# Linear attention and a gated feed-forward layer on one core: weight sums, two loads and the order of block 1 moved to other places

## The chip, the cores and the metric

The kernel runs on one core of a Trainium2 chip. The metric is the device time of one execution in microseconds (us), lower is better. The engines named here are PE (TensorE: matmuls and transposes through the array), DVE (VectorE), ACT (ScalarE), POOL (GpSimd, which also issues DMAs on a queue of its own, q0 in the profile) and SP (SyncE, which only issues DMAs, on queue q1).

## The reference

```
attention, batch 8, heads 8, sequence 576, head size 64:
  phi(x) = [relu(x) * cos(w_pos), relu(x) * sin(w_pos)]      (128 features)
  kv = sum over s of phi(k)_s v_s^T ;  z = sum over s of phi(k)_s
  x  = (phi(q) kv) / (phi(q) z + 1e-6)
feed-forward on the 8 * 576 = 4608 rows of x:
  h = x @ w_in            (512 -> 2048)
  y = (h * sigmoid(1.702 h)) @ w_out      (2048 -> 512)
```

Inputs and output are float32; the kernel multiplies in bfloat16.

## The kernel before

**Blocks.** Each batch b is one block. Its first 512 positions go through the feed-forward layer in the block itself; the last 64 positions of every batch are kept in `xt` and `gt` and done together behind the last block. The instructions of each engine are written out by hand in the order in which they run, so whatever stands ahead on an engine's list and waits holds back all that follows on that engine.

**What one block does.** `load_q`, `load_kv` bring q, k and v of a batch into the single buffers `qf`, `kf`, `vf` (about 1.2 MB each). DVE makes phi(q) into `qn` (`trig_q`, L185, ten instructions) and SP turns it into `qT` by five transposing DMAs (`qturn_dma`, L219). DVE makes phi(k) into `kr` (`trig`, L169, eighteen instructions) and copies v into `vt` (`vcopy`, L193). `kv_next` multiplies `kr` and `vt` on PE (L237, 72 small matmuls) and DVE takes the result out into `kvs` (L245). `x_next(b, c)` makes the attention output of one chunk c of the positions: `num_mm` on PE (L310, needs `kvs` and `qT`), `num_div` on DVE (L321, L323, L325), and a transposing DMA into `xT`. `mm1(b, fc)` is the first matmul of the layer (L365, four matmuls of 512 columns, sixteen fc to a block), followed by the activation on ACT (L371).

**The second matmul of the layer.** Block 0 uses plain matmuls (`mm2`, L419). From block 1 on it is done by seven products in place of eight (`wino_mm`, L502). Those need four sums of quarters of w_out, kept in `wsum` (`w_sums`, L440 to L443: t1, t2, t3, nt4), and sums of quarters of the activations (`g_sums`, L465 to L471). t1 reads the first half of w_out alone, the other three read the second half too.

**Order around the change.** In block 0, POOL issues the loads q of batch 1, the third quarter of w_out, v of batch 1 and the last quarter of w_out. DVE makes phi(k) and phi(q) of batch 1 and half of `vcopy`; ACT does the rest of both. SP issues the five transposes of `qT`, then q, k and v of batch 2, in that order on one queue. PE runs `mm2(0, ...)`, and from the middle of its last quarter on `kv_next`, `num_mm(0)` to `num_mm(4)` of batch 1. Then DVE makes the four weight sums in one go, ahead of all its work for batch 2.

In block 1 the first five `mm1` are done in `start_block`, so the loop starts at fc 5. Blocks 2 to 6 place `kv_next` for the next batch in front of `mm1(b, 14)` and `x_next(b + 1, 0)` in front of the products. Block 1 alone places `vcopy` behind the second step of the products, `kv_next` behind step 3, and the five `x_next` behind steps 4, 5, 6, 8 and 10.

Of the kernel before, what the change touches and what calls it, by code (L numbers as in the profile page):

```python
# [15 lines left out]
SUB = mybir.AluOpType.subtract  # L16
# [4 lines left out]
def kernel(  # L21
# [9 lines left out]
    nc = tc.nc  # L31
# [25 lines left out]
    def src_of(src, b, i0=0, i1=NI):  # L57
        return src[b, 2 * i0:2 * i1].rearrange("(i hh) (p j) d -> (hh p) i (j d)", hh=2, j=NS)

    qf = one.tile([128, 2560], F32, name="qf")  # L60
    kf, vf = [one.tile([128, NI, S], F32, name=n) for n in ("kf", "vf")]
# [62 lines left out]
    def load(t, src, b, eng=nc.gpsimd):  # L124
        eng.dma_start(out=t, in_=src_of(src, b))

    def load_chunks(t, src, b, eng):
        eng.dma_start(out=t[:, 0:2048].rearrange("p (h e) -> p h e", h=H),
                      in_=src[b, :, 0:512, :].rearrange("h (p c) d -> p h (c d)", c=4))
        eng.dma_start(out=t[0:64, 2048:2560].rearrange("p (h e) -> p h e", h=H),  # L130
                      in_=src[b, :, 512:S, :].rearrange("h p d -> p h d"))

    def load_q(b, eng=nc.gpsimd):
        load_chunks(qf, q, b, eng)
# [11 lines left out]
    def load_kv(b):  # L146
        load(kf, k, b, nc.sync)
        load(vf, v, b, nc.sync)
# [12 lines left out]
    def trig(dst, src, j, act=False, eng=nc.vector):  # L161

        i = src[:, :, ts(j, 64)]
        for cs, w in enumerate((cosw, sinw)):
            o = dst[:, j, :, ts(cs, 64)]
            if act is True or (act == "sin" and cs == 1):
                nc.scalar.activation(o, i, AF.Relu, scale=w[:, j:j + 1])
            else:
                eng.tensor_scalar(o, i, 0.0, w[:, j:j + 1], op0=MAX, op1=MUL)  # L169
# [6 lines left out]
    def trig_q(c, act=False):  # L176
        n = 128 if c < 4 else 64
        i = chunk(qf, c)
        for cs, w in enumerate((cosw, sinw)):
            o = qn[0:n, c, :, ts(cs, 64)]  # L180
            sc = w[0:n, NS + c:NS + c + 1]
            if act:
                nc.scalar.activation(o, i, AF.Relu, scale=sc)
            else:
                nc.vector.tensor_scalar(o, i, 0.0, sc, op0=MAX, op1=MUL)  # L185

    def vcopy(i0=0, i1=NI, act=False):
        o = vt[:, :, i0:i1, 0:64].rearrange("p j i e -> p i j e")
        i = vf[:, i0:i1].rearrange("p i (j e) -> p i j e", e=64)
        if act:  # L190
            nc.scalar.activation(o, i, AF.Copy)
        else:
            nc.vector.tensor_copy(o, i)  # L193
# [23 lines left out]
    def qturn_dma(c):  # L217
        n = 128 if c < 4 else 64
        nc.sync.dma_start_transpose(out=qT[:, :, c * 128:c * 128 + n],  # L219
                                    in_=qn[0:n, c].rearrange("p h f -> p (h f)"))  # L220
# [3 lines left out]
    def kv_open(i0=0, i1=NI, n=65):  # L224
        t = pat.tile([128, 2, 512], F32, name="at")
        for i in range(i0, i1):
            st["kv", i] = t[:, :, ds((i - i0) * n, n)]
        st["ps", i0] = t[:, :, 0:(i1 - i0) * n]
        if i0 == 0:
            st["kvs"] = small.tile([128, 2, NI, VW], BF16, name="kvs", bufs=2)  # L230

    def kv_mm(i0, i1, rhs, col, n):
        for i in range(i0, i1):
            for j in range(NS):
                for hh in range(2):
                    r = slice(hh * 64, hh * 64 + 64)
                    nc.tensor.matmul(st["kv", i][:, hh, ds(col, n)], kr[r, j, i, :], rhs(r, i, j),  # L237
                                     start=(j == 0), stop=(j == NS - 1))
# [4 lines left out]
    def kv_evac(i0, i1, n=65):  # L243
        o = st["kvs"][:, :, i0:i1, 0:n]
        nc.vector.tensor_copy(o, st["ps", i0].rearrange("p hh (i e) -> p hh i e", e=n))  # L245
# [85 lines left out]
    def x_open(b):  # L331
        x[b] = xpool.tile([128, KC, MT], BF16, name="xT")
# [40 lines left out]
    def mm1(b, fc):  # L373
        mm1_part(b, fc, 0, MT)
        gelu(fc)
# [38 lines left out]
    def mm2(b, t, lo, hi, c0=0, c1=d_model, end=False):  # L414
# [6 lines left out]
        if hi == FC:  # L421
# [10 lines left out]
    wt = {n: wsum[:, i].rearrange("p (f d) -> p f d", f=HF)  # L432
          for i, n in enumerate(("t1", "t2", "t3", "nt4"))}
    wq = {(k, n): w_out_sb[:, ts(k, HF), ts(n, HD)] for k in range(2) for n in range(2)}
    sg = {n: sums[:, i].rearrange("p (f t) -> p f t", f=HF)
          for i, n in enumerate(("s1", "s2", "s3", "s4"))}

    def w_sums():
        tt = nc.vector.tensor_tensor
        tt(wt["t1"], wq[0, 1], wq[0, 0], op=SUB)  # L440
        tt(wt["t2"], wq[1, 1], wt["t1"], op=SUB)
        tt(wt["t3"], wq[1, 1], wq[0, 1], op=SUB)
        tt(wt["nt4"], wq[1, 0], wt["t2"], op=SUB)  # L443

    def main_blk(i, qd):

# [11 lines left out]
    def g_sums(names, h, of=MAIN):  # L458

        tt = nc.vector.tensor_tensor  # L460
        a_blk, to = of
        o = {n: to[n][:, ts(h, 4)] for n in to}
        for n in names:
            if n == "s1":
                tt(o[n], a_blk(1, h), a_blk(1, h + 2), op=ADD)  # L465
            elif n == "s2":
                tt(o[n], o["s1"], a_blk(0, h), op=SUB)  # L467
            elif n == "s3":
                tt(o[n], a_blk(0, h), a_blk(1, h), op=SUB)  # L469
            else:  # L470
                tt(o[n], a_blk(0, h + 2), o["s2"], op=SUB)  # L471
# [117 lines left out]
    def kv_next():  # L589
        kv_open()  # L590
        kv_mm(0, 4, vt_rhs, 0, 65)
        kv_evac(0, 4)
# [122 lines left out]
    load_wout(3)  # L715
    for j in range(NS):
        trig(kr, kf, j)
    for fc in range(8, FC):
        mm1(0, fc)
    mm1_tail_first(0)  # L720
    mm1_tail_first(1)
    for c in range(5):
        trig_q(c, act=(c > 2))
        qturn_dma(c)
    vcopy(0, 2)
    vcopy(2, 4, act=True)
    load_q(2, nc.sync)
    load_kv(2)
    for g in range(2):
        for t in range(4):  # L730
            mm2(0, t, 4 * g, 4 * g + 4)
# [21 lines left out]
    def kv_operands(b):  # L753
        for j in range(NS):
            trig(kr, kf, j)
        if b > 2:
            vcopy()

    def x_next(b, c):
        num_mm(c)  # L760
        num_div(c)
        xturn_dma(b, c)


    w_sums()

    for b in range(1, B):
        nb = b + 1 if b + 1 < B else None
        f0 = 5 if b == 1 else 0
        for fc in range(f0, FC):  # L770
            if nb is not None and fc == f0:
                for c in range(5):
                    trig_q(c)
                    qturn_dma(c)
            if nb is not None and fc == f0 + 1:
                kv_operands(nb)

                if nb + 1 < B:
                    load_q(nb + 1, nc.sync)
            if fc == 12:  # L780
                g_sums(("s3",), 0)
                g_sums(("s3",), 1)
                g_sums(("s1", "s2", "s4"), 0)
            if fc == 14 and nb is not None and b > 1:
                kv_next()
            mm1(b, fc)
        if nb is not None:
            x_open(nb)
            if b > 1:
                x_next(nb, 0)  # L790
            g_sums(("s1", "s2"), 1)
            at = {2 * p + 1: [p + 1] for p in range(4)} if b > 1 else {4: [0], 5: [1], 6: [2], 8: [3], 10: [4]}
            wino_open()
            for p in range(7):
                for c in range(2):
                    wino_mm(p, c)
                    s = 2 * p + c
                    if c == 1:
                        wino_after(b, p)
                    if s == 3 and b == 1:  # L800
                        kv_next()
                    for c2 in at.get(s, ()):
                        x_next(nb, c2)
                        if c2 == 3 and nb + 1 < B:
                            load_kv(nb + 1)
                    if s == 1:
                        g_sums(("s4",), 1)
                        if b == 1:
                            vcopy()
            continue  # L810
        for fc in range(FC):
            mm1_tails(fc)
            if fc == 0:
                g_sums(("s1", "s2", "s4"), 1)
        for h in range(2):
            g_sums(("s1", "s2"), h, TAIL)
        g_sums(("s3",), 0, TAIL)
        g_sums(("s3",), 1, TAIL)
        wino_open()
        for p in range(7):  # L820
            for c in range(2):
                wino_mm(p, c, TAIL)
            wino_after(None, p, end=True)
            if p == 1:
                g_sums(("s4",), 0, TAIL)
                g_sums(("s4",), 1, TAIL)
        wino_open(last=True)
        for p in range(7):
            for c in range(2):
                wino_mm(p, c)  # L830
                if p == 6:
                    wino_last(b, c)
            wino_after(b, p, end=True)
# [30 lines left out]
```

## Time and profile before

| what | value |
|---|---|
| time, median of 3 runs (lowest, highest) | 286.5 us (285.62, 286.88) |
| the profiled execution: its own time, its span | 288.89 us, 287.2 us |
| PE busy, share of the span | 273.7 us, 95% |
| DVE, ACT, POOL busy | 185.7, 128.3, 41.4 us |
| mean granted clock of PE | 0.987 |
| DMA packets on q1 (SP), q0 (POOL), share of 16 engines | 56.8%, 20.2% |

Busy times are sums over an engine's instructions. The span runs from the first to the last instruction; the execution's own time has what lies around it as well. "Idle before" is time in which an engine had nothing to run ahead of a group, and the name behind the arrow ended that wait. A DMA's time to landing runs from its issue until its data is there.

### The profile page before, as it was taken

The numbers are of one execution on the slowest core, as the hardware profiler recorded it, in microseconds if no ns is written. First come the engines' busy times: TensorE is split into PE (matmuls) and PEld (weight loads), VectorE is DVE, ScalarE is ACT, GpSimd is POOL, SyncE is SP. The second block draws the span as 40 slices with busy tenths as digits, with TensorE's granted clock in tenths as the row PEclk, the third lists the DMA queues.
The fourth block names the chain that finished last, engine by engine and source line by source line (L and its number), as shares of the span: only waits on it lengthen the run. The fifth ranks groups of instructions, "written<-read, shape, count | busy, mean of one in ns | idle before, by whom it ended". The sixth has DMA issues, their size and how long they took to land.

```text
span 287.2 us, 6573 instructions
## 1 busy us (share of the span) xinstructions
PE 273.7 (95%) x2700; PEld 191.5 (67%) x2700; DVE 185.7 (65%) x451; ACT 128.3 (45%) x225; POOL 41.4 (14%) x70
## 2 busy tenths in 40 slices
PE   8999999996698989999999999999999999999995
PEld 2675645854594559757975797579757975568884
DVE  4835434799585798796779678967897711516111
ACT  6967543672014722364236413641374137773221
POOL 5680003200112001300130013001300130000320
PEclk9999999999599999999999999999999999999999
DMA  7999999999349999999699979987994430000143
GB/s 238 245 212 295 270 257 204 350 296 202 103 64 251 290 183 168 292 264 236 112 305 221 217 148 314 256 212 107 290 279 54 109 119 2 0 0 2 47 138 110
DMA packets 73661, 53.57 MB, mean 187 GB/s; under 512 B 52736, under 2 KB 63488, under 8 KB 73632
## 3 DMA queue, kind: packets, MB, share of 16 engines
q1 hardware_dynamic: 67504, 36.97, 56.8%
q0 software_dynamic: 6128, 16.19, 20.2%
q8 instruction: 21, 0.34, 0.5%
q14 instruction: 8, 0.07, 0.1%
HBM read 36.70 MB, written 9.44 MB: 161 GB/s over the span
## 4 chain that ended last, share of the span: by engine, by line
PE 77%; DVE 10%; DMA 9%; issue 1%; ACT 1%; POOL 0%; DVEq 0%; SPq 0%
PE mm L502 32%; PE mm L365 29%; DMA kf<-in_k_dram 5%; PE mm L396 4%; PE mm L419 4%; PE at L237 3%; DVE kr L169 3%; PE at L310 3%; DMA sums<-in_v_dram 2%; DMA out_dram<-ysb 2%; DVE qn L185 1%; DVE vt L193 1%; DVE sums L469 1%; PE mm L388 1%; DVE sums L467 1%
## 5 line engine op out<-in xcount | busy, mean ns | idle before, releaser
L365 PE MATMUL mm<-xT,w_in 128*128 128x512 bf16 (+1 forms) x592 | 113.7, 349 | 1.5 <-DMA xT<-xn 1.4
L371 ACT ACTIVATE g<-mm 128x512 bf16<-128x512 f32 x128 | 75.6, 598 | 41.2 <-PE mm L365 41.2
L365 PEld LDWEIGHTS <-w_in 128*128 128x128 bf16 x592 | 60.1, 113 | 48.3 <-issue 1.7
L502 PEld LDWEIGHTS <-sums 128*128 128x128 bf16 x448 | 42.6, 98 | 5.0
L508 POOL DMA_DIRECT2D out_dram<-ysb x24 | 17.5, 729 | 165.2 <-DVE inv L323 96.8
L502 PE MATMUL mm<-wsum,sums 128*128 128x256 bf16 x336 | 40.9, 276 | 0.0
L502 PEld LDWEIGHTS <-g 128*128 128x128 bf16 x336 | 32.2, 98 | 3.8
L169 DVE TENSOR_SCALAR kr<-kf,cosw 128x256 bf16<-128x256 f32 x69 | 24.2, 350 | 10.0 <-DMA kf<-in_k_dram 10.0
L325 DVE TENSOR_TENSOR xn<-at,inv 128x512 bf16<-128x512 f32 x39 | 27.0, 691 | 1.3
L502 PE MATMUL mm<-w_out_sb,g 128*128 128x256 bf16 x224 | 26.4, 272 | 0.0
L169 DVE TENSOR_SCALAR kr<-kf,sinw 128x256 bf16<-128x256 f32 x68 | 23.1, 339 | 0.0
L517 ACT ACTIVATE kept_u<-mm 128x512 f32<-128x512 f32 (+1 forms) x9 | 4.9, 550 | 33.7 <-PE mm L502 16.9
L517 ACT ACTIVATE kept_p<-mm 128x512 f32<-128x512 f32 (+1 forms) x17 | 9.7, 572 | 22.6 <-PE mm L502 22.6
L185 DVE TENSOR_SCALAR qn<-qf,cosw 128x512 bf16<-128x512 f32 (+1 forms) x33 | 16.3, 494 | 4.0 <-DMA qf<-in_q_dram 4.0
L321 DVE TENSOR_SCALAR den<-at 128x8 f32<-128x8 f32 x36 | 5.9, 163 | 17.4 <-PE at L310 17.4
L310 PEld LDWEIGHTS <-qT 128*128 128x128 bf16 x312 | 14.6, 98 | 3.4 <-issue 1.0
L569 ACT ACTIVATE ysb<-mm 128x512 f32<-128x512 f32 x6 | 3.6, 597 | 29.3 <-PE mm L502 29.3
L310 PE MATMUL at<-kvs,qT 128*128 128x65 bf16 x312 | 15.9, 194 | 0.8 <-DVE kvs L245 0.8
L237 PEld LDWEIGHTS <-kr 64*128 64x128 bf16 x576 | 10.3, 98 | 8.2 <-issue 6.5
L185 DVE TENSOR_SCALAR qn<-qf,sinw 128x512 bf16<-128x512 f32 (+1 forms) x33 | 15.6, 473 | 0.0
L237 PE MATMUL at<-vt,kr 64*128 64x65 bf16 x504 | 9.7, 197 | 5.5 <-DVE vt L193 5.5
L419 PE MATMUL mm<-w_out_sb,g 128*128 128x512 bf16 x64 | 14.8, 379 | 0.0
(120 smaller groups left out, 264.7 us busy)
## 6 DMA issues: line engine op xcount, KB each, us to landing
kf<-in_k_dram SPq DMA_DIRECT2D x6, 1152.0 KB, 6.5
vf<-in_v_dram SPq DMA_DIRECT2D x6, 1152.0 KB, 11.8
qf<-in_q_dram SPq DMA_DIRECT2D x6, 1024.0 KB, 6.5
out_dram<-ysb POOLq DMA_DIRECT2D x24, 256.0 KB, 6.5
w_out_sb<-in_moe_w_out_dram POOLq DMA_DIRECT2D x4, 512.0 KB, 17.6
kf<-in_k_dram POOLq DMA_DIRECT2D x1, 1152.0 KB, 13.2
vf<-in_v_dram POOLq DMA_DIRECT2D x1, 1152.0 KB, 20.7
w_in<-in_moe_w_in_dram POOLq DMA_DIRECT2D x2, 512.0 KB, 10.2
```

The costliest lines, as they stand in the source:

```text
L169: eng.tensor_scalar(o, i, 0.0, w[:, j:j + 1], op0=MAX, op1=MUL)
L185: nc.vector.tensor_scalar(o, i, 0.0, sc, op0=MAX, op1=MUL)
L237: nc.tensor.matmul(st["kv", i][:, hh, ds(col, n)], kr[r, j, i, :], rhs(r, i, j), start=(j == 0), stop=(j == NS - 1))
L310: nc.tensor.matmul(ps[:, h // 4, ds((h % 4) * 65, 65)], qT[:, h, ts(c, 128)], kvs_of(h), start=not eps_too, stop=(not eps_too or h % 4 == ...
L325: nc.vector.tensor_tensor(xn, pv[:, :, :, 0:64], inv.unsqueeze(3).to_broadcast([128, 2, 4, 64]), op=MUL)
L365: nc.tensor.matmul(hp[fc][:, t0:t1], wcol(kc, fc), x[b][:, kc, t0:t1], start=(kc == 0), stop=(kc == KC - 1))
L371: nc.scalar.activation(gT[fc // 4][:, fc % 4], hp.pop(fc), AF.Gelu_apprx_sigmoid)
L396: nc.tensor.matmul(hps[:, 64:B * 64], wcol(kc, fc), xt[:, kc, 64:B * 64], start=(kc == 0), stop=(kc == KC - 1))
L419: nc.tensor.matmul(yp[b, t, c0][:, c0:c1], w, w_out_sb[:, fc, c0:c1], start=(fc == 0), stop=(fc == FC - 1))
L502: nc.tensor.matmul(bank[to][c], lhs, rhs, start=opens, stop=(fc == HF - 1), skip_group_check=True)
L508: eng.dma_start(out=dst[:, 2 * i + c0:2 * i + c1, ts(n, HD)], in_=t[:, c0:c1])
L517: nc.scalar.activation(o, i, AF.Identity)
```

## The change

The four weight sums move ahead into block 0, in three parts. t1 goes behind the eighteen phi(k) instructions. The other three sums are cut into halves: the first half goes behind DVE's phi(q), the second behind DVE's half of `vcopy`. The loads of k and v of batch 2 leave SP's queue; POOL issues k behind the phi(k) instructions of batch 1, and v behind the two `vcopy`. In block 1 `vcopy` follows phi(k) as in the later blocks, `kv_next` stands between `mm1(1, 15)` and the products (the later blocks have it two `mm1` earlier), and the five `x_next` stand behind the steps 1, 3, 5, 7 and 9 of the products (the later blocks have the first ahead of them and the others behind 1, 3, 5 and 7).

```diff
-    def w_sums():
+    def w_sum_1():
+        nc.vector.tensor_tensor(wt["t1"], wq[0, 1], wq[0, 0], op=SUB)
+
+    def w_sums(h):
         tt = nc.vector.tensor_tensor
-        tt(wt["t1"], wq[0, 1], wq[0, 0], op=SUB)
-        tt(wt["t2"], wq[1, 1], wt["t1"], op=SUB)
-        tt(wt["t3"], wq[1, 1], wq[0, 1], op=SUB)
-        tt(wt["nt4"], wq[1, 0], wt["t2"], op=SUB)
+        o = {n: wt[n][:, ts(h, 4)] for n in wt}
+        w = {n: wq[n][:, ts(h, 4)] for n in wq}
+        tt(o["t2"], w[1, 1], o["t1"], op=SUB)
+        tt(o["t3"], w[1, 1], w[0, 1], op=SUB)
+        tt(o["nt4"], w[1, 0], o["t2"], op=SUB)
...
     for j in range(NS):
         trig(kr, kf, j)
+    load(kf, k, 2)
+    w_sum_1()
     for fc in range(8, FC):
         mm1(0, fc)
...
     for c in range(5):
         trig_q(c, act=(c > 2))
         qturn_dma(c)
+    w_sums(0)
     vcopy(0, 2)
     vcopy(2, 4, act=True)
+    load(vf, v, 2)
+    w_sums(1)
     load_q(2, nc.sync)
-    load_kv(2)
...
     def kv_operands(b):
         for j in range(NS):
             trig(kr, kf, j)
-        if b > 2:
-            vcopy()
+        vcopy()
...
-    w_sums()
...
             x_open(nb)
             if b > 1:
                 x_next(nb, 0)
+            else:
+                kv_next()
             g_sums(("s1", "s2"), 1)
-            at = {2 * p + 1: [p + 1] for p in range(4)} if b > 1 else {4: [0], 5: [1], 6: [2], 8: [3], 10: [4]}
+            first = 1 if b > 1 else 0
+            at = {2 * p + 1: [p + first] for p in range(5 - first)}
...
-                    if s == 3 and b == 1:
-                        kv_next()
...
                     if s == 1:
                         g_sums(("s4",), 1)
-                        if b == 1:
-                            vcopy()
```

## Prediction

> **What bounds the kernel now.** I read the page's busy times first, then PE's waits, PE's timeline around block 1, the chain of waits there, and the landings of the DMAs that feed it. The page gives the shares of the chain that ended last:
>
> ```profile
> PE 77%; DVE 10%; DMA 9%; issue 1%; ACT 1%; POOL 0%; DVEq 0%; SPq 0%
> ```
>
> PE sets the time, so only PE's idle and slow stretches can be won. Between 60 us and the end PE waits four times (the waits of PE, 60 to 110 us):
>
> ```profile
> PE at L237 <- DVE vt L193: 5.5, 2, 4.8
> PE mm L365 <- DMA xT<-xn: 1.4, 1, 1.4
> PE at L310 <- DVE kvs L245: 0.8, 1, 0.8
> ```
>
> PE's timeline shows where (start, length, then the wait in brackets):
>
> ```profile
> 65.54 3.66 PE L502 MATMUL mm<-w_out_sb,g 128*128 128x256 bf16 x32
> 74.05 2.16 PE L237 MATMUL at<-vt,kr 64*128 64x65 bf16 x72 [4.85 <-DVE vt L193]
> ...
> 88.66 12.25 PE L365 MATMUL mm<-xT,w_in 128*128 128x512 bf16 x56 [1.41 <-DMA xT<-xn]
> 101.52 1.26 PE L237 MATMUL at<-vt,kr 64*128 64x65 bf16 x72 [0.61 <-DVE vt L193]
> ...
> 105.39 0.40 PE L310 MATMUL at<-kvs,qT 128*128 128x65 bf16 x8 [0.76 <-DVE kvs L245]
> ```
>
> The big one is block 1: PE has made two of seven products and stands 4.85 us for v of batch 2. The chain of waits tells why:
>
> ```profile
> 53.99 1.22 DVE wsum L440
> ...
> 57.51 1.22 DVE wsum L443
> 58.73 3.96 DVE qn L185 x10
> 62.69 2.41 DVE kr L169 x10
> ...
> 72.64 1.36 DVE vt L193
> 74.00 0.04 issue
> 74.05 2.16 PE at L237 x72
> ```
>
> DVE has no gap there from 54 to 74 us; the weight sums stand ahead of all of it, and the copy of v stands last. The wait also costs clock, as the stretches of time show (PE busy is the second figure, PEclk the granted clock):
>
> ```profile
> 70.00:74.00 4.00, 0.00 (x0) 0.00 (x0) 3.93 (x6) 0.00 (x0) 0.00 (x0) 0.68 0.84 263
> 74.00:78.00 4.00, 3.95 (x83) 3.33 (x83) 1.29 (x2) 0.00 (x0) 0.74 (x1) 0.50 0.21 70
> ```
>
> The 72 small matmuls take 2.16 us there and 1.19 in the chain at 131.07, eight of L502 1.82 and then 0.87, eight of L310 0.39 and then 0.24: 0.97 + 0.95 + 0.15 = 2.07 us lost to the clock.
>
> **What can be won at most.** 4.85 + 2.07 in block 1, 1.41 at the start of block 2 and 0.61 + 0.76 inside it: 9.7 us.
>
> **Weight sums.** t1 needs the first half of w_out, landed at 31.34. DVE ends phi(k) at 31.38 and idles 3.99 us until q of batch 1 lands, so 1.22 us is hidden. The first halves (three of 1024 elements, like L465's 0.61 to 0.70: 2.0 us) run from the landing of the third quarter at 37.97 to 40.0, inside the 3.00 us that DVE idles for v; hidden. The second halves wait for the last quarter, 23.73 + 19.6 = 43.33, and end at 45.35; queued behind them is the copy of `kvs` that began at 45.24, and `num_mm(0)` waits for it: 0.1 us. What is taken from 53.99 to 58.65 is 4.66 us of DVE.
>
> **k and v on POOL's queue.** POOL stands idle from 24.3 to 47.1, so the issues (0.7 us each) hold nobody up: k at 31.4, v behind ACT's copy at 42.0. On the queue they follow the last quarter of w_out. Block 0's eight outputs, issued from 47.1, now queue behind them; before, the last of them landed at 59.2, and their four buffers are written again only by block 1's first output, near 74, so 6 us more cost nothing. On SP's queue the next transposes no longer stand behind k and v. The loads' price is in the DMA engines. Alone, k of batch 1 took 3.1 us (landed 26.55, the load ahead of it 23.45) and v 2.85 (40.82 after 37.97): 5.95 us now lie ahead of, or among, the five transposes and the load of q of batch 2, which have stayed on SP. Three rows on these (the first `qT` transpose from 36.35, q from 46.84, and the traffic of q1 between 46.9 and 48.2):
>
> ```profile
> qT<-qn SPq DMA_TRANSPOSE x1, 7.9
> ...
> qf<-in_q_dram SPq DMA_DIRECT2D x1, 1024.0 KB, 7.2
> ...
> q1 hardware_dynamic: 78, 0.02, 8.9%
> ```
>
> q landed at 54.04, just as DVE came free, so every us by which it lands later is a us for DVE's chain. The engines stood nearly empty for 1.2 us at 46.9 to 48.2; if k and v fill that, q slips 5.95 - 1.2 = 4.75 us, if not 5.95; if they only take turns that nobody else used, nothing. In the stretch 37.97 to 53.00 the DMA share was 1.14, full, so I take a value near the middle row: q lands at 58.5, bounds 54.1 and 60.0. The Trainium skill speaks against this part of the change (DMA: Bandwidth & Descriptors, Issuing engines are not separate DMA queues): transfers issued from different engines run on the same 16 DMA engines, and another issuer saves only issue time. The share of 1.14 agrees.
>
> **The transposes' delay.** `num_mm(0)` ran at 46.01 with its `qT` there since 44.28, and the next at 46.68 with 45.20: slack 1.7 and 1.5. If k and v pass all five transposes (the first landed 0.95 behind the last w_out; k and v end at 43.33 + 5.95 = 49.3), the first lands at 50.2 and PE stands 4.3 us, with about 2 us of slow clock behind. If they take turns, 0 to 1 us. I take 0.5. The rows speak for some waiting: the transpose issued at 36.35 had no packet before 40.0, beside q0's loads. The Trainium skill (DMA: Bandwidth & Descriptors, Queues, rings and completion order) says that a DMA engine goes round between its queues packet by packet; by it the delay is near 0, and the end is the one forecast here, since q of batch 2 decides.
>
> **Block 1's new order.** From q's landing Q, DVE needs 3.96 (phi(q)) + 4.72 (phi(k)) + 1.27 (v) = 9.95 us until `kv_next` may run, then 3.24 for five activation sums and 0.70 for `kvs`: `num_mm(0)` at Q + 13.95. PE ends `mm1(1, 15)` at 65.54 and would reach `num_mm(0)` 1.19 + 1.75 later: 68.5 (with the transposes' 0.5, 69.0). With Q = 58.5 it is 72.45, 3.95 later than without any wait: 2.9 us ahead of `kv_next`, 1.05 ahead of `num_mm(0)`. These gaps are shorter than the 4.85 that halved the clock and longer than the 1.41 that did not; I take no clock loss, bound 2 us. The Trainium skill (TensorE: Matmul & The Clock Gate, Part 1) puts the limit at about 3.4 us of idleness; by it the loss is also none.
>
> **Block 2.** Its wait for `xT` (1.41) goes, since the fourth chunk moves from step 8 to 7 and the block is not behind; bound 0.4 left. k of batch 3 is issued about 3.0 us ahead of block 2 (six steps of 0.87 and two L310 groups of 0.24 follow, less the 2.7 from L310 to that issue in block 2, 140.08 to 142.75), as before (85.86 against 88.66); there it took 9.5 us and left 0.61 + 0.76. I keep 1.0 of the 2.8, bounds 0 and 1.8.
>
> **Sum.** 9.7 - 3.95 - 1.0 = 4.75 us, on the profiled execution's 288.89 (span 287.2 and 1.7 around it) 284.1; that execution lies 2.4 above the median, so on 286.5 it is 281.8.
>
> **Rivals.**
> - *The loads fit in.* q lands by 55.5: `num_mm(0)` at 69.0 to 69.5, win 9.7 - 1.0 - 0.5 to 1.0, so 7.7 to 8.2: 278.3 to 278.8, and 277.3 if nothing is left in block 2. For it: empty engines at 46.9 and slack of the transposes. Against: share 1.14. Chance 0.17.
> - *k and v pass the transposes.* PE stands 4.3 us in block 0 with 2 us of clock; it reaches `num_mm(0)` at 68.5 + 6.3 = 74.8, q lands at 60 (73.95), PE decides: win 9.7 - 6.3 - 1.0 = 2.4, 284.1. For it: no packet before 40.0. Chance 0.16.
> - *Slower: transposes and loads hold each other up.* From 61.0 to 63.5, where v of batch 2 and the transposes shared the engines, they moved 156 GB/s, against 402 between 58.0 and 60.5 for loads alone and 268 for transposes alone (44 to 46). That is half of the pace. From 40 us on there would be 5.95 us of loads and 4.3 us of transposes (four and a half, 0.95 from landing to landing between 44.28 and 46.15): 10.2 us would take 20, until 60, and q landed 4.7 behind the last transpose (54.04 against 49.33): 65. The win is gone when `num_mm(0)` comes 8.7 us late, at 77.2, so with q at 63.3; with q at 65 it comes at 78.95, 10.45 late: 9.7 - 10.45 - 1.0 = -1.75, 288.2. Against: before, such mixtures lasted 2 to 3 us and then cleared. Chance 0.20.
> - *No change*: the same with q between 61.9 and 64.7. Chance 0.10.
>
> **How the numbers follow.** The forecast has 0.37. Faster takes it, the first two rivals: 0.70; same 0.10; slower 0.20. About 0.5% (1.4 us) is what a measurement of this kernel can tell from no change. The range leaves out the best half of the first rival and the worse half of the slower one: 278 to 288.5; for the forecast alone 280 to 284.
>
> **What would show it.** Right: the wait of 4.85 for `vt` in block 1 is gone or under 3.5, four weight sums lie before 45.5, and DVE waits 3 to 5 us for `qf` near 55 to 59. `num_mm(0)` of batch 2 near 72. Wrong: PE idle ahead of L310 between 46 and 53 by more than 1 us, q of batch 2 landed after 63, or phi(q) of batch 2 starting at 54 without a wait.

## The result, and the profile after

The changed kernel takes 295.04 us (median of 4 runs, 294.46 to 297.3), the kernel before beside it 286.56 (285.62 to 286.88). The ratio is 1.0316 [1.0255, 1.0377]: slower by 3.2%, where 281.8 us had been forecast. The profiled execution took 297.3 us with a span of 295.6; against the 287.2 of before that is 8.4 us more. Each ratio, here and below, rests on the runs within 1.5% of the fastest of their kernel and stands with its 95% interval; medians and ranges take in all runs. In the new listing the weight sums are L439 and L446 to L448 and the products L507; the other lines shown in this section kept their numbers.

The shares of the chain that ended last, by engine and by line:

```profile
PE 71%; DMA 19%; DVE 4%; ACT 2%; POOL 2%; SPq 1%; issue 0%; POOLq 0%; DVEq 0%
PE mm L507 32%; PE mm L365 28%; DMA qT<-qn 9%; DMA qf<-in_q_dram 6%; DMA kf<-in_k_dram 4%; PE mm L396 4%; PE at L310 3%; PE at L237 2%; DVE kr L169 2%; ACT qn L167 1%; PE mm L419 1%; POOL qn L169 1%; ACT kr L167 1%; PE at L342 0%; SPq L219 0%; DVE vt L193 0%
```

DVE fell from 10% to 4%, as the change intends, and DMA rose from 9% to 19%; 9% of the span is one transpose `qT<-qn` that took 26 us. The waits of PE between 40 and 110 us are one line (total, times, longest):

```profile
PE at L310 <- DMA qT<-qn: 15.8, 2, 11.3
```

None of the waits shown for before is left, and one new wait is larger than all of them. PE's timeline (start, length, wait in brackets) shows where it is, and the old places without their brackets:

```profile
50.77 0.62 PE L310 MATMUL at<-kvs,qT 128*128 128x65 bf16 x8 [4.47 <-DMA qT<-qn]
51.20 1.04 PE L419 MATMUL mm<-w_out_sb,g 128*128 128x512 bf16 x2
63.59 0.62 PE L310 MATMUL at<-kvs,qT 128*128 128x65 bf16 x8 [11.34 <-DMA qT<-qn]
...
84.05 1.26 PE L237 MATMUL at<-vt,kr 64*128 64x65 bf16 x72
87.00 0.41 PE L310 MATMUL at<-kvs,qT 128*128 128x65 bf16 x8
98.69 11.60 PE L365 MATMUL mm<-xT,w_in 128*128 128x512 bf16 x53
```

`num_mm(0)` of batch 1 waits 4.47 us for the first transpose of `qT` and `num_mm(1)` 11.34 for the second. The five transposes landed at 50.73, 63.54, 64.99, 65.84 and 66.44; before, at 44.28, 45.20, 46.15, 48.83 and 49.33. PE also runs slowly behind these waits (eight of L310 at 0.62 are the sign): from the first `num_mm` at 50.77 to the fourth at 69.54, less the 11.34 us of waiting, are 7.43 us, and the same matmuls took 5.13 before (46.01 to 51.14), 2.3 less. The balance closes: 15.8 + 2.3 lost, 9.7 won (all the waits and slow matmuls of before), 8.4 to the worse.

What the DMA engines did is in the stretches (us, then PE, PEld, DVE, ACT and POOL busy, granted clock, DMA share, GB/s):

```profile
40.00:44.00 4.00, 4.00 (x20) 1.67 (x17) 1.53 (x3) 1.17 (x1) 0.75 (x1) 1.00 1.02 310
46.00:57.00 11.00, 1.78 (x12) 0.57 (x10) 1.15 (x4) 0.60 (x1) 1.09 (x2) 0.69 1.27 74
57.00:63.00 6.00, 0.00 (x0) 0.00 (x0) 0.00 (x0) 0.00 (x0) 0.00 (x0) 0.50 1.11 179
```

For eleven microseconds the share is 1.27 while 74 GB/s move. The share adds up the times of all packets, so it tells that packets were under way, not that bytes moved. The queues in the first two of these stretches (packets, MB, share; q0 carries POOL's loads, q1 SP's transposes), first 40 to 44 us with the two DMAs whose issue falls into it (that of the transpose began at 37.56) and their time to landing:

```profile
q0 software_dynamic: 277, 1.17, 93.2%
q1 hardware_dynamic: 270, 0.07, 9.0%
...
vf<-in_v_dram POOLq DMA_DIRECT2D x1, 1152.0 KB, 20.7
qT<-qn SPq DMA_TRANSPOSE x1, 26.0
```

and 46 to 57 us:

```profile
q1 hardware_dynamic: 1224, 0.30, 81.7%
q0 software_dynamic: 122, 0.51, 45.5%
```

In the first stretch the queues come out packet for packet, 277 to 270, but a packet of the loads has 4.2 KB (1.17 MB over 277) and one of the transposes 256 bytes: the transposes get 68 packets a microsecond. In the kernel before, between 44 and 46 us and with nothing beside them, q1's line reads

```profile
q1 hardware_dynamic: 2154, 0.54, 122.5%
```

which is 1077 a microsecond. The second stretch is something else. The share divided by the packets gives the mean time of one: 117 ns for a transpose packet (0.817 x 16 engines x 11 us / 1224) where it was 21 ns in the first stretch and 18 ns alone, and 660 ns for a load packet that took 215 in the first. Both means have become three to six times as long at once, but by a part of the packets only: in the trace's packet records the median of this stretch is still 18 ns for a transpose packet and 190 for a load packet, while 38% of the transpose packets took 150 ns or more and 24% of the load packets over 1 us.

Such slow packets are not the mixture's alone. In the kernel before, between 46 and 47 us, no load had a packet under way (one packet of 16 KB on the instruction queue aside), and q1's line reads

```profile
q1 hardware_dynamic: 492, 0.12, 279.8%
```

which is 91 ns a packet (the median again 18, the longest 1.7 us). There it passed within about 2 us: the fourth transpose landed 2.7 us behind the third, where the earlier ones landed about 0.9 apart. In the changed kernel it lasts until the loads are through, near 63.

The weight sums came out as forecast. DVE's timeline:

```profile
31.65 1.23 DVE L439 TENSOR_TENSOR wsum<-w_out_sb 128x2048 bf16<-128x2048 bf16 x1
...
45.38 0.70 DVE L245 CAST kvs<-at 128x520 bf16<-128x520 f32 x1 [0.26 <-PE at L237]
```

### The profile page after: what moved, and what is told of

It is laid out like the page before. It is cut to its first block, busy times and chain, and to the rows that moved or that the text cites. A ratio compares the mean times of both kernels' runs of the same rounds, so it can differ in the third digit from the quotient of the medians.

```text
span 295.6 us, 6578 instructions
## 1 busy us (share of the span) xinstructions
PE 273.8 (93%) x2700; PEld 191.0 (65%) x2700; DVE 185.9 (63%) x454; ACT 128.4 (43%) x225; POOL 42.9 (15%) x72
## 4 chain that ended last, share of the span: by engine, by line
PE 71%; DMA 19%; DVE 4%; ACT 2%; POOL 2%; SPq 1%; issue 0%; POOLq 0%; DVEq 0%
PE mm L507 32%; PE mm L365 28%; DMA qT<-qn 9%; DMA qf<-in_q_dram 6%; DMA kf<-in_k_dram 4%; PE mm L396 4%; PE at L310 3%; PE at L237 2%; DVE kr L169 2%; ACT qn L167 1%; PE mm L419 1%; POOL qn L169 1%; ACT kr L167 1%; PE at L342 0%; SPq L219 0%; DVE vt L193 0%
## 5 line engine op out<-in xcount | busy, mean ns | idle before, releaser
L507 PEld LDWEIGHTS <-sums 128*128 128x128 bf16 x448 | 42.5, 98 | 4.7
L507 PE MATMUL mm<-wsum,sums 128*128 128x256 bf16 x336 | 39.8, 272 | 0.0
L507 PEld LDWEIGHTS <-g 128*128 128x128 bf16 x336 | 32.0, 98 | 3.6
L310 PE MATMUL at<-kvs,qT 128*128 128x65 bf16 x312 | 16.1, 195 | 16.0 <-DMA qT<-qn 15.8
L310 PEld LDWEIGHTS <-qT 128*128 128x128 bf16 x312 | 14.5, 99 | 19.4 <-DMA qT<-qn 17.2
L507 PE MATMUL mm<-w_out_sb,g 128*128 128x256 bf16 x224 | 26.6, 272 | 0.0
L419 PE MATMUL mm<-w_out_sb,g 128*128 128x512 bf16 x64 | 16.6, 410 | 0.0
L532 DVE TENSOR_TENSOR ysb<-mm,kept_p 128x512 f32<-128x512 f32 x13 | 8.9, 688 | 8.6 <-DMA out_dram<-ty 4.6
L470 DVE TENSOR_TENSOR sums<-g 128x1024 bf16<-128x1024 bf16 x14 | 9.6, 684 | 7.1 <-ACT g L371 7.1
```

Source lines behind the costliest of these rows:

```text
L310: nc.tensor.matmul(ps[:, h // 4, ds((h % 4) * 65, 65)], qT[:, h, ts(c, 128)], kvs_of(h), start=not eps_too, stop=(not eps_too or h % 4 == ...
L419: nc.tensor.matmul(yp[b, t, c0][:, c0:c1], w, w_out_sb[:, fc, c0:c1], start=(fc == 0), stop=(fc == FC - 1))
L507: nc.tensor.matmul(bank[to][c], lhs, rhs, start=opens, stop=(fc == HF - 1), skip_group_check=True)
```

## The experiments

Ten kernels were run, each in rounds beside the kernel before. The theory: k and v of batch 2, placed on POOL's queue among the transposes of `qT`, cost all of the loss, by a collapse of the DMA engines' pace in which loads and transposes hold each other up; the weight sums and the new order gain. The rivals, as they came up: sums and order are at fault; POOL's queue is bad for these loads wherever they stand; the price goes by the bytes that pass the transposes; the loss is only the turns that are taken.

**1. k and v back on SP's queue**, all else as changed.

```diff
-    load(kf, k, 2)
     w_sum_1()
...
-    load(vf, v, 2)
     w_sums(1)
     load_q(2, nc.sync)
+    load_kv(2)
```

> The changed kernel, with k and v of batch 2 back on SP's queue behind q of batch 2; weight sums and block 1's order stay changed. Theory M (plain loads on POOL's queue and transposing DMAs on SP's queue hold each other up while both are in flight; the 15.8 us for which PE waited for qT in the changed kernel are all from that): no wait of PE for qT in block 0, and the 9.7 us of waits and slow clock of before are won less about 2 us, because k lands near 60.7 and v near 63.7: 279 us, bounds 277.5 to 281. Rival S (the earlier weight sums hold up the copy of kvs, or PE's new order waits as well): PE still waits 3 us or more ahead of L310 in block 0, 285 us or more.

Measured: 281.22 us (280.77 to 281.57) against 287.2, ratio 0.9776 [0.9731, 0.9822]. The waits of PE behind the start:

```profile
PE at L237 <- DVE vt L193: 1.9, 1, 1.9
...
PE at L310 <- DVE kvs L245: 0.8, 1, 0.8
```

No wait for `qT`, and 2.2% won. The time lies 0.2 us over the range expected, since k now landed at 61.20, DVE stood 2.88 us for it, and PE 1.90 and 0.75 in block 1. That sums and order were at fault has fallen.

**2. The two loads alone**, on the kernel before.

```diff
         trig(kr, kf, j)
+    load(kf, k, 2)
...
     vcopy(2, 4, act=True)
+    load(vf, v, 2)
     load_q(2, nc.sync)
-    load_kv(2)
```

> The kernel before with the two loads alone moved to POOL's queue as in the change; weight sums and block 1's order as before. Theory M: PE waits about 16 us for qT in block 0 with about 2 us of slow clock, and block 1 keeps its 4.85 us wait for vt, as DVE starts its chain later by the same amount: 303 us, bounds 299 to 306. Rival S (sums and order take part in the loss): 296 us or less.

Measured: 303.51 us against 287.2, ratio 1.0576 [1.0508, 1.0644]. The waits of PE, 40 to 110 us:

```profile
PE at L310 <- DMA qT<-qn: 15.2, 2, 11.5
PE at L237 <- DVE vt L193: 4.8, 1, 4.8
```

The wait of the changed kernel is there without sums or order, and block 1's old wait for `vt` stands beside it. The loads alone lose 16 us; the other two parts give some of it back.

**3. The loads on POOL, but behind the last transpose.** POOL copies one element of the last columns of `qT` first, which holds its queue until they have landed.

```diff
-    load(kf, k, 2)
     w_sum_1()
...
     vcopy(2, 4, act=True)
+    nc.gpsimd.tensor_copy(gate[0:1, 2:3], qT[0:1, 0, 512:513])
+    load(kf, k, 2)
     load(vf, v, 2)
```

> The changed kernel, with POOL holding k and v of batch 2 back, by a copy of one element, until the last of the five qT transposes has landed (near 49.3); both loads stay on POOL's queue, ahead of block 0's outputs. Theory M: the transposes land as before (44.3 to 49.3), no wait of PE for qT, k and v land by 60: 279 us, bounds 277.5 to 281. Rival Q (POOL's queue carries these loads badly whenever they run): k or v takes over 12 us, DVE waits for them, 285 us or more.

Measured: **278.57 us** (278.53 to 278.61) against 287.2, ratio **0.9685 [0.9633, 0.9736]**: 3.1% faster than before, and the fastest of all kernels run. All waits of PE in the whole execution:

```profile
PE mm L586 <- DVE warm L80: 1.2, 1, 1.2
PE mm L251 <- DVE kr L169: 1.0, 2, 0.6
PE mm L299 <- DVE xh L291: 0.2, 1, 0.2
```

All three lie in the first 16 us, and stood there before too, the second as a wait of 0.2. From there on PE never waits, the granted clock is 1.000, and the span is 276.9. The transposes landed between 43.97 and 49.00, 0.3 us earlier than before. k was issued at 49.66 and landed at 56.94, v 50.43 and 60.83; q on SP landed at 53.17. The same bytes on the same queue, some 18 us later for k and 8 for v, cost nothing. That POOL's queue is bad for them has fallen.

**4. k early on POOL, v back on SP.**

```diff
-    load(vf, v, 2)
     w_sums(1)
     load_q(2, nc.sync)
+    load(vf, v, 2, nc.sync)
```

> The changed kernel with v of batch 2 back on SP's queue behind q; k stays on POOL's queue, issued near 32. In the changed kernel k landed at 46.4, so it is in flight together with the transposes for about 3 us only. Theory M: the first transposes land about 3 us later (47.5, 48.5), PE waits 1.5 to 3 us for qT: 281 us, bounds 279.5 to 283. Rival B (the price goes with the bytes that come ahead; k is half of them): PE waits about 8 us, 287 us, bounds 285 to 290.

Measured: 282.25 us (282.06 to 282.73), ratio 0.9816 [0.9771, 0.986]. Its wait for the transposes:

```profile
PE at L310 <- DMA qT<-qn: 0.6, 1, 0.6
```

Half of the bytes pass the transposes and cost 0.6 us of waiting, not 8, and less than the 1.5 to 3 expected too. The transposes landed at 46.93 to 53.58, late by 2.6 to 4.3, which PE's slack mostly covers. The price does not go by the bytes alone.

**5. The weight sums alone**, on the kernel before: `w_sum_1()` and `w_sums(0)`, `w_sums(1)` at the places of the change, loads and order as before.

```diff
+    w_sum_1()
...
+    w_sums(0)
     vcopy(0, 2)
     vcopy(2, 4, act=True)
+    w_sums(1)
...
-    w_sums()
```

> The kernel before with the weight sums alone moved into block 0 in three parts; loads and block 1's order as before. DVE comes free at 54.1 in place of 58.7, but k of batch 2 lands only near 60.7 to 61.2 on SP's queue, so phi(k) starts 1.5 to 2 us earlier than before, not 4.7. PE's wait for vt falls from 4.85 to about 3 us, with or without the 2.07 us of slow clock: 283.5 us, bounds 282.5 to 285.5. Rival (the sums were the whole of the wait): 280 us or less.

Measured: 286.0 us (ten runs, 282.53 to 289.22, the widest spread of all) against 287.38, ratio 0.9889 [0.9857, 0.9922]. The ratio leaves out the four longest of the ten (286.88 and more); by the medians of all runs the gain is 0.5%. The time lies 0.5 us over the range expected. PE in block 1:

```profile
71.79 2.03 PE L237 MATMUL at<-vt,kr 64*128 64x65 bf16 x72 [2.65 <-DVE vt L193]
```

Of the 4.66 us taken from DVE only 2.2 came off the wait. DVE stands 2.32 us for k of batch 2, which lands at 60.31 behind q on SP's queue, so the load takes over from the sums as what comes last; and the wait, though shorter, still halves the clock (0.50 from 72 to 74 us). Most of the spread is this clock: the three runs with a mean granted clock of 1.000 took 282.53 to 284.03 us, the seven with 0.992 to 0.994 took 285.37 to 289.22.

**6. The order of block 1 alone**, on the kernel before: sums in the old place, loads on SP.

```diff
-        if b > 2:
-            vcopy()
+        vcopy()
...
+            else:
+                kv_next()
...
-            at = {2 * p + 1: [p + 1] for p in range(4)} if b > 1 else {4: [0], 5: [1], 6: [2], 8: [3], 10: [4]}
+            first = 1 if b > 1 else 0
+            at = {2 * p + 1: [p + first] for p in range(5 - first)}
```

> The kernel before with block 1's new order alone; loads and the four weight sums stay where they were (the sums cut as in the change). DVE reaches phi(q) at 58.7, v's copy ends near 68.7, so PE waits about 3 us ahead of kv_next and 1 us ahead of num_mm(0), and the waits of block 2 go: 282.5 us, bounds 281 to 284.5. Rival (the order needs the early sums, kv_next just waits in another place): 285.5 us or more.

Measured: 283.85 us (283.14 to 284.04), ratio 0.9876 [0.9853, 0.99], inside the range. PE waits 3.45 us for `vt` and 0.75 for `kvs`, without a slow clock behind in the profiled run (granted 1.000; the three others had 0.991 to 0.994); block 2 has no wait. Experiments 5 and 6 bring 1.1% (or 0.5%, see there) and 1.2%, both together (experiment 1) 2.2%, and with the loads in a harmless place 3.1%.

**7. v on POOL where the change has it, k on SP behind q.**

```diff
-    load(kf, k, 2)
     w_sum_1()
...
     load_q(2, nc.sync)
+    load(kf, k, 2, nc.sync)
```

> The changed kernel with k of batch 2 back on SP's queue behind q; v alone stays on POOL's queue, issued near 42, when the transposes (from 36 on) are already queued. Theory O (it is the load that is issued after the transposes have been queued that interleaves with them and slows both; a load queued ahead of them runs through first): v takes over 10 us to land, PE waits 6 us or more for qT, 287 us or more, up to 296. Rival B (1.2 MB cost the same whichever load it is; k alone on POOL cost PE 0.6 us): PE waits 0.5 to 2 us, 281 to 283.5 us.

Measured: 284.67 us (283.67 to 286.49), ratio 0.9903 [0.9876, 0.993]. The waits of PE, 40 to 110 us:

```profile
PE at L237 <- DVE vt L193: 2.8, 1, 2.8
PE at L310 <- DMA qT<-qn: 2.3, 1, 2.3
```

v, issued at 42.67, landed after 7.2 us, where it took 20.7 behind k. So v in that place doesn't bring the collapse by itself: the first two transposes came through (44.67, 45.59), the third came at 52.09. q landed at 61.16, and the rest of the loss is DVE's. Neither side's numbers were met; those of the price by bytes were nearer.

**8. Both loads early, back to back.** v of batch 2 goes into memory that is free then (that of `sums`), so it needn't wait for `vcopy` and is issued right behind k, at 32.47.

```diff
+    vf2 = sums.rearrange("p n e -> p (n e)").bitcast(F32)[:, 0:NI * S].rearrange("p (i e) -> p i e", i=NI)
...
     load(kf, k, 2)
+    load(vf2, v, 2)
...
-    load(vf, v, 2)
...
-        vcopy()
+        vcopy(src=vf2 if b == 2 else vf)
```

> The changed kernel with v of batch 2 in a buffer of its own (the sums' memory, which is free until block 1), so that POOL issues it right behind k, near 32.5, ahead of the transposes; all else as in the change. Theory O: k and v run through first, v lands near 49.3, the first transpose near 50, PE waits about 4 us for qT with up to 2 us of slow clock, q of batch 2 lands near 59: 283.5 us, bounds 281.5 to 286. Rival C (any load and transposes in flight together collapse, whichever came first): v takes over 15 us, PE waits over 10 us, 292 us or more.

Measured: 285.78 us (285.45 to 286.29), ratio 0.9954 [0.9935, 0.9973]. The queues between 42 and 47 us:

```profile
q0 software_dynamic: 422, 1.86, 97.3%
q1 hardware_dynamic: 421, 0.11, 9.9%
```

and PE's wait:

```profile
PE at L312 <- DMA qT<-qn: 4.2, 2, 3.4
```

(L312 is L310 of the others, two lines down.) All of the bytes of the change are ahead of or among the transposes and cost 4.2 us, not 15.8. While the loads last, the queues come out packet for packet (422 to 421), at 389 GB/s between 42 and 46 us; k landed at 45.90, v at 49.08, the first transpose 0.4 us later, and all five by 54.81. This is the prediction's case in which k and v pass the transposes. Its 4.3 us is met partly by chance: it meant one wait, and here are two, of 3.35 and 0.89.

**9. v on POOL only when the first transpose has landed.**

```diff
     vcopy(2, 4, act=True)
+    nc.gpsimd.tensor_copy(gate[0:1, 2:3], qT[0:1, 0, 0:1])
     load(vf, v, 2)
```

> The changed kernel, k early on POOL's queue as in the change, v on POOL's queue too, but POOL holds it back, by a copy of one element, until the first of the five qT transposes has landed (near 46.9, as with k alone). v then joins the transposes 2 to 5. Theory T (the collapse needs v to arrive while k's tail and the first transpose are still in flight, at 43 to 47): v takes 7 us or less, PE waits 3 us or less for qT, 284 us, bounds 281 to 286. Rival R (any load that joins transposes already queued collapses with them): v takes over 10 us, PE waits over 6 us, 288 us or more.

Measured: 286.18 us (285.33 to 287.79), ratio 0.9966 [0.9945, 0.9987].

```profile
PE at L310 <- DMA qT<-qn: 4.8, 3, 3.5
```

v, issued at 47.95, landed in 6.7 us, as expected of turns, and there is no long collapse. But the wait is 4.8, not the 3 or less expected: 1.01, 0.28 and 3.52 us for three of the chunks, and the time is 0.2 us over the range. The transposes behind the first are now those that get few turns: 47 packets of q1 beside 168 of q0 between 52 and 54 us, and the last transpose landed at 57.93.

**10. Half of v on POOL, half on SP behind q.**

```diff
-    load(vf, v, 2)
+    nc.gpsimd.dma_start(out=vf[:, 0:2], in_=src_of(v, 2, 0, 2))
     w_sums(1)
     load_q(2, nc.sync)
+    nc.sync.dma_start(out=vf[:, 2:4], in_=src_of(v, 2, 2, 4))
```

> The changed kernel with half of v of batch 2 (heads 0 to 3) on POOL's queue at its place in the change and the other half on SP's queue behind q; k early on POOL. Theory P (in the collapsed state loads and transposes go at a slow pace set by v's packets, 256 of them in 17 us): half the packets, PE waits about 8 us in place of 15.8, q of batch 2 lands near 64, 288.5 us, bounds 286.5 to 291. Rival Z (the collapse is set off by v's arrival and lasts as long whatever its size): 293 us or more. Rival N (half of v drains before the engines fall out of step): PE waits 2 us or less, 284 us or less.

Measured: 292.82 us (291.82 to 294.18), ratio 1.0202 [1.0163, 1.0241].

```profile
PE at L310 <- DMA qT<-qn: 10.0, 2, 6.0
```

Between the two numbers that would have told whether the collapse lasts as long as there are bytes of v or runs its own course: 10.0 us of waiting with half the bytes, 0.6 with none and 15.8 with all. The half took 14.9 us to land. That the collapse needs all of v has fallen; how its length goes with the bytes stays open.

## Why the prediction was wrong, step by step

**The step that failed is "The transposes' delay".** It took 0.5 us and bounded it by 4.3 us and 2 us of clock. It was 15.8 us and 2.3 of clock. Two of the signs that the prediction named for being wrong are there: PE idle ahead of L310 (4.47 us until 50.77), and q of batch 2 landed after 63 (at 71.58). Experiment 2 has this loss without the rest of the change, experiments 1 and 3 have the rest without the loss.

- *The bound.* The 4.3 us assumed that at worst the loads go first, each at its own pace (5.95 us together). Experiment 8 is that case and gave 4.2. What lay outside was that both slow down together. The forecast had that as its slower rival, from the 156 GB/s of a mixture in the kernel before, which made 20 us of 10.2. Its mechanism, that they hold each other up, was the right one and its size too small: 74 GB/s for 11 us, with q of batch 2 issued only at 64.84. The rival also let it act on q of batch 2 and priced the transposes by the q that follows them, while the wait that decided was that of `num_mm(1)` in block 0, with 1.5 us of slack.
- *The skill's rule at that step.* The Trainium skill (DMA: Bandwidth & Descriptors, Queues, rings and completion order) has the engines go round between the queues packet by packet. The counts of the profile's packets agree while k's load runs (277 to 270, and 422 to 421 in experiment 8), and not later: in the collapse they are 1224 to 122. The conclusion drawn from it, a delay near 0, was wrong: a turn of 256 bytes against one of 4.2 KB leaves the transposes a sixteenth of their pace (68 of 1077 packets a microsecond) while a load is queued. Equal turns are no equal shares.
- *What the collapse needs.* Shown: k alone on POOL costs 0.6 us of waiting for `qT`, v alone 2.3, v held until the first transpose 4.8, both early 4.2, k early with half of v joining 10.0, with all of v 15.8. So in these runs it came only with k ahead and v joining at 42 us, while k's tail (landed 46.44 in the changed kernel) and the transposes were under way. Why some packets of both queues then take so long stays open; that the engines fall out of step, each transpose waiting for its slowest, is only a guess, which no run here tests.

**"k and v on POOL's queue".** Q was put at 58.5 with bounds of 54.1 and 60.0, and came out at 71.58, because its issue on SP waits behind the transposes. The stretch that was read there as nearly empty (46.9 to 48.2 in the kernel before) was not free: the fourth transpose was under way, with packets of up to 1.7 us, and landed at 48.83. The rule cited there from the same page (Issuing engines are not separate DMA queues) fits in its first half: loads issued on POOL and transposes issued on SP held each other up (experiment 2). Its second half, that another issuer saves only issue time, leaves out what was measured, since the queue also sets what a load stands behind: on POOL, behind the transposes, k was issued 0.7 us later than on SP behind q (49.66 against 48.93) and landed 4.3 us earlier (56.94 against 61.20, experiments 3 and 1). As it was, q decided nothing: DVE was free for it only at 72.39, and PE reached `num_mm(0)` at 87.00 without a wait.

**"Weight sums": right.** t1 at 31.65, first halves 37.79 to 39.7, second halves 43.23 to 45.13, the copy of `kvs` at 45.38 (before 45.24), against a forecast cost of 0.1 us.

**"Block 1's new order" and "What can be won at most": right as far as tested.** In experiment 3, where nothing disturbs them, `num_mm(0)` runs at 68.66, forecast as 68.5 if no wait is left, and 10.3 us of span are gone where 9.7 were named; by the medians, against 287.2, it is 8.6 us. The "no clock loss" behind waits of 1 to 3 us was not safe: experiment 7 has a slow clock behind 2.77 us. The sum Q + 13.95 should read 13.89 (9.95 + 3.24 + 0.70), on which nothing hangs.

**"Block 2".** 1.0 us was kept for it; nothing was left in the changed kernel, nor in experiments 1, 3 and 6. The `xT` wait went with the order: experiment 6 has lost it, experiment 5 (1.73 us) has not.

**The sum.** With the 15.8 + 2.3 put in (the 0.5 was not in it, since q was to decide), no loss in block 1 and none kept in block 2, it is 9.7 - 18.1 = -8.4. Experiment 3 measures 278.57, within the 278.3 to 278.8 of the first rival, that the loads fit in. The number is partly luck: with nothing left in block 2, as there, that rival gave 277.3. But the win was there, and the place of the two loads gave it away.

## What to carry to other kernels

A free queue and an idle issuing engine don't make a load free: ask which small-packet transfers (here transposing DMAs) are in flight in that window and how much slack their readers have, since each of their packets then waits its turn behind a large one. Where the load isn't needed soon, let its issuer wait for the last transpose; here a copy of one element ahead of the two loads turned 3.2% slower into 3.1% faster. Bound the delay of a mixture by runs of that mixture, not by the sum of what its parts take alone.

## What the runs showed of the hardware that had not been expected

- Loads and transposes together can collapse: for 11 us 74 GB/s move at a DMA share of 1.27, against 402 for loads alone (58 to 60.5 us) and 268 for transposes alone (44 to 46) in the kernel before. The mean transpose packet takes 117 ns, not 18, while the median stays at 18. In the kernel before the last transposes do it alone, for about 2 us (46 to 48, 72 GB/s at a share of 1.46).
- The clock of PE fell to 0.50 behind waits of 2.65 us (experiment 5) and 2.77 (experiment 7, 72 matmuls of L237 in 2.16 us), and stayed at 1.00 behind one of 3.45 (experiment 6, 1.26 us). The Trainium skill (TensorE: Matmul & The Clock Gate, Part 1) puts the limit at about 3.4 us of idleness in a window that runs freely; the two shorter waits are below it, so the measurement decides: a wait of 2.65 us can already cost the clock, and one of 3.45 need not.
- The length of the wait alone does not decide. The traces record the clock in stretches, and the slow ones last 3.41 us (experiments 5 and 7), 6.83 (the kernel before) or 17.07 (the changed kernel), so the clock changes in steps of 3.41 us. In the step ahead of a slow stretch PE was busy for 0.77 us (experiment 5, 68.59 to 72.01) and 1.21 (the kernel before, 67.99 to 71.40). Experiment 6's wait is spread over two steps, with 1.33 and 2.05 us busy (64.17 to 71.00), and the clock stayed. Where a wait falls among the steps thus matters, and it is not the same in every run, as the granted clocks of experiment 5 (1.000 in three runs of ten) suggest.
